# Two smaller transfers near the end, and tiles of their own for the last sums, in a decode-attention kernel

## The chip, the cores and the metric

The kernel runs on one core of a Trainium2 chip. The time is device microseconds (us) of that core; lower is better. A "run" is one timed execution. The profile is one execution with the hardware profiler on; its span is about 1.8 us shorter than the time that is reported for the same execution (1341.8 us against 1343.62 us for the kernel before).

Names: PE is TensorE, DVE is VectorE, ACT is ScalarE, SP is the engine that issues the transfers (all but one of the two of the output). Landing times come from the landing records of the trace, sixteen for a transfer; a transfer has "landed" with the last of them. L576 is line 576 of the kernel in question.

## The reference

```python
x = A_x                                          # [4, 1, 1024], bf16
g = sigmoid((x * gate_w).sum(-1, keepdims=True))
q = (x @ wq) -> [4, 32 heads, 1, 128]
p = softmax(q . k_cache * 128**-0.5)             # k_cache, v_cache: [4, 32, 8192, 128]
a = (p . v_cache) -> [4, 1, 4096] @ wo           # wo: [4096, 1024]
b = x + sigmoid(x . w_r) * (silu(x @ w_gate) * (x @ w_up)) @ w_down   # one token is chosen of one
out = g * a + (1 - g) * b
```

The two caches are 268 MB each. Everything else is small beside them.

## The kernel before

The caches are read in 32 "pairs" each, of 8 MB (four heads of one batch). A ring of five slots of 4 MB in SBUF takes them; a pair needs two slots. The order is: K pairs 0 to 31, V pair d eight places behind K pair d, and at the end the eight V pairs 24 to 31 alone, with the rows of `wo` behind them. PE multiplies each V pair in 64 matmuls into `o_ps` (four banks of PSUM). After every second V pair ACT and DVE sum the four banks into `OS`; the next pair may not overwrite `o_ps` before. `finish` then sends `OS` through eight small matmuls, and `scaled` writes the result to `OT`.

```python
    def load_pair(src, n, apart=False):
        a = slots(2)
        if a + 1 < NS and not apart:             # the two slots lie side by side: one transfer of 8 MB
            ...
            nc.sync.dma_start(out=flat[:, lo:lo + 2 * n], in_=src)
            return [...]
        for i, half in enumerate(halves):        # else two of 4 MB
            nc.sync.dma_start(out=half[:, 0:n], in_=src[:, i * n:(i + 1) * n])
...
    def v_pair(d):
        ...
        if d < ND - 1:                           # ND = 32
            vs = load_pair(vv, RING, apart=d >= ND - 3)
        else:                                    # pair 31: 2 x 2 MB and 4 x 1 MB
            vs = [ring[:, slots(1)] for _ in range(2)]
            for half, cuts in ((0, 2), (1, 4)):
                for c in range(cuts):
                    ...
        for u in range(4 * RD):                  # 16 steps of 4 matmuls
            n, z = divmod(u, 4)
            vn = vs[n // JT]
            for w in range(4):
                j0 = CJ * (n % JT) + 16 * z + 4 * w
                nc.tensor.matmul(o_ps[row:row + NM, w, :], lhsT=PB[...], rhs=vn[:, j0 * Dh:(j0 + 4) * Dh],
                                 start=(u == 0), stop=(u == 4 * RD - 1), skip_group_check=True)
            if u == 1:
                flush()                          # finish of the sums before
...
    A_ps.append(S0)      # after K pair 31: the tile of the scores, four banks, becomes
                         # output accumulators (banks 0, 1), oT (2), row sums and LT rows (3)
...
    # the end: wo blocks 2 to 7; acc(n) is bank n of A_ps[0]
    res = turned(Bn, D)
    nc.vector.tensor_copy(out=res[:, 0:NB], in_=acc(0))
    nc.sync.dma_start(out=out2[:, 0:NB], in_=res[:, 0:NB])
    nc.scalar.copy(out=res[:, NB:D], in_=acc(1))
    nc.scalar.dma_start(out=out2[:, NB:D], in_=res[:, NB:D])
```

Waits are set by the framework in which the kernel is written.

## Time and profile before

| | kernel before |
|---|---|
| median of the first 3 runs | 1345.1 us (1344.78 to 1345.45) |
| span of the profiled execution | 1341.8 us |
| HBM read, mean rate | 575.68 MB, 429 GB/s |
| PE / DVE busy | 79% / 48% |
| last landing of an input | 1337.35 us |

From the page of the kernel before, the DMA row (busy tenths in 40 slices of the span) and the total:

```profile
DMA  9999999999999999999999999999999999999997
...
HBM read 575.68 MB, written 0.01 MB: 429 GB/s over the span
```

The transfers never pause before the last slice (9 in 39 of 40), so bytes over rate set nearly the whole time. The rate by slice is 415 to 443 GB/s in those 39 and 326 GB/s in the last.

What is left to argue about is the end. The waits of PE of the kernel before, from 1235 us to the end (total us, times, longest):

```profile
PE o_ps L536 <- DMA ring<-in_A_v_cache_dram: 10.9, 4, 6.5
PE o_ps L536 <- DVE OS L556: 3.1, 1, 3.1
PE S_ps L285 <- DMA ring<-in_A_wo_dram: 1.2, 2, 0.6
PE S_ps L285 <- DVE LT L382: 0.7, 2, 0.4
PE S_ps L285 <- DVE OT L576: 0.3, 1, 0.3
```

After 1259 us PE hardly waits for data (0.9 us for pair 31 and 1.2 us for `wo`). The timeline of the kernel before over its last 15 us (start us, length, engine, line, operation; in brackets idle time before it and what ended it):

```profile
1330.34 0.24 DVE L576 SCALAR_TENSOR_TENSOR OT<-S_ps,sgb,rinv 128x8 bf16<-128x8 f32 x1 [2.93 <-PE S_ps L564]
1330.63 1.89 PE L285 MATMUL S_ps<-ring,LT 128*4 128x512 bf16 x8 [0.33 <-DVE OT L576]
1332.36 0.32 PE L380 MATMUL S_ps<-OT,identb 128*32 128x8 bf16 x16
1332.76 0.19 DVE L382 CAST LT<-S_ps 128x32 bf16<-128x32 f32 x1 [2.18 <-PE S_ps L380]
1333.00 5.34 PE L285 MATMUL S_ps<-ring,LT 128*4 128x512 bf16 x24 [0.32 <-DVE LT L382]
1338.38 0.68 DVE L622 CAST TB<-S_ps 4x512 bf16<-4x512 f32 x1 [5.43 <-PE S_ps L285]
...
1339.09 0.57 ACT L624 CAST TB<-S_ps 4x512 bf16<-4x512 f32 x1 [14.03 <-DVE TB L622]
```

PE stands 0.33 us for the scaling of `OT`; ACT copies its half of the output only after DVE.

### The profile page before, as it was taken

The page shows a single profiled execution, that of the slowest core. Times are in us where ns is not written, and L with a number is a line of the kernel's source. Part 1 is how long each engine was busy: PE and PEld are TensorE (multiplying, and loading weights), DVE is VectorE, ACT ScalarE, POOL GpSimd, SP SyncE. Part 2 cuts the span into 40 slices and gives each one's busy share as a digit, 9 for nine tenths or more (in the row PEclk, how much of TensorE's full clock was granted, in tenths as well). Part 3 has the DMA queues.
Part 4 walks back from the last instruction along what each step waited for, and adds up shares of the span by engine and source line. Part 5 has one row for each costly group of instructions (what it writes and reads, how often), then busy time and mean ns, then how long its engine had stood idle before and what let it go on. Part 6 is the DMA issues. An engine that isn't in the chain of part 4 may idle for free.

```text
span 1341.8 us, 6893 instructions
## 1 busy us (share of the span) xinstructions
PE 1055.8 (79%) x4608; PEld 138.4 (10%) x1396; DVE 639.0 (48%) x386; ACT 63.3 (5%) x94; POOL 71.4 (5%) x209
## 2 busy tenths in 40 slices
PE   2565877887788788787879778789697879887888
PEld 0000000001011010101001010101011011111111
DVE  2555988556544347455436256646145556000001
ACT  0000000200000000100000000100000000100000
POOL 2000000100000001000000000100000000100000
PEclk9777989898989899888889889889898889889999
DMA  9999999999999999999999999999999999999997
GB/s 415 438 430 435 435 438 423 443 430 424 434 436 427 443 434 422 443 428 432 438 429 434 434 432 432 436 436 424 430 433 433 436 428 442 432 421 437 426 425 326
DMA packets 14314, 576.13 MB, mean 429 GB/s; under 512 B 1598, under 2 KB 1606, under 8 KB 2252
## 3 DMA queue, kind: packets, MB, share of 16 engines
q1 hardware_dynamic: 14276, 575.69, 99.5%
q8 instruction: 23, 0.38, 0.1%
q14 instruction: 7, 0.06, 0.0%
q10 hardware_dynamic: 8, 0.00, 0.0%
HBM read 575.68 MB, written 0.01 MB: 429 GB/s over the span
## 4 chain that ended last, share of the span: by engine, by line
DMA 65%; DVE 24%; PE 11%; issue 0%; ACT 0%; SPq 0%; DVEq 0%
DMA ring<-in_A_k_cache_dram 51%; DVE TB L452 21%; PE o_ps L536 8%; DMA ring<-in_A_v_cache_dram 7%; DMA ring<-in_A_wo_dram 4%; DMA ring<-in_B_w_gate_dram 3%; DVE OS L556 2%; PE S_ps L457 1%; PE S_ps L285 1%; PE o_ps L319 0%; PE S_ps L564 0%; DVE PT L493 0%; DVE mx L479 0%; DVE OT L576 0%; ACT OS L552 0%
## 5 line engine op out<-in xcount | busy, mean ns | idle before, releaser
L452 DVE STREAM_TRANSPOSE TB<-ring 128x2048 uint32<-128x2048 uint32 x256 | 568.2, 2278 | 472.0 <-DMA ring<-in_A_k_cache_dram 453.9
L457 PE MATMUL S_ps<-TB,Z 128*128 128x512 bf16 x2048 | 531.0, 414 | 189.5 <-DVE TB L452 181.9
L536 PE MATMUL o_ps<-ring,PB 128*64 128x512 bf16 x2048 | 462.1, 388 | 52.6 <-DMA ring<-in_A_v_cache_dram 46.3
L457 PEld LDWEIGHTS <-Z 128*128 128x128 bf16 x512 | 53.0, 104 | 652.6 <-issue 652.6
L536 PEld LDWEIGHTS <-PB 128*64 128x64 bf16 x512 | 57.2, 112 | 451.7 <-issue 451.1
L556 DVE SCALAR_TENSOR_TENSOR OS<-o_ps,mE,OS 128x512 f32<-128x512 f32 x48 | 35.6, 741 | 142.1 <-ACT OS L552 141.0
L512 POOL COPY PB<-PT 32x256 bf16<-32x256 bf16 x64 | 38.9, 608 | 721.5 <-PE o_ps L536 528.5
L510 ACT COPY PB<-PT 32x256 bf16<-32x256 bf16 x64 | 39.6, 619 | 255.7 <-PE o_ps L536 249.9
L434 POOL COPY Z<-qa 32x4 bf16<-32x4 bf16 x128 | 25.6, 200 | 458.2 <-PE S_ps L457 431.0
L552 ACT ACTIVATE OS<-o_ps,mE 128x512 f32<-128x512 f32 x16 | 11.0, 687 | 584.7 <-PE o_ps L536 584.7
L488 ACT ACTIVATE TB<-S_ps,mx 128x2048 bf16<-128x2048 f32 x4 | 7.9, 1967 | 322.2 <-DVE mx L485 322.2
L285 PE MATMUL S_ps<-ring,hT 128*4 128x512 bf16 x56 | 14.6, 430 | 5.4 <-ACT TB L488 5.4
L243 PE MATMUL S_ps<-identb,x 6*128 6x6 bf16 x8 | 0.6, 195 | 22.1 <-DMA x<-in_gate_w_dram 22.1
L285 PE MATMUL S_ps<-ring,LT 128*4 128x512 bf16 x64 | 14.6, 379 | 2.3 <-DMA ring<-in_A_wo_dram 1.2
L564 PEld LDWEIGHTS o_ps<-selg,OS 128*128 128x128 f32 x88 | 11.5, 191 | 9.3 <-issue 8.8
L493 DVE STREAM_TRANSPOSE PT<-TB 128x2048 bf16<-128x2048 bf16 x4 | 9.2, 2312 | 6.4 <-ACT TB L488 6.4
L479 DVE TENSOR_REDUCE mx<-S_ps 128x1 f32<-128x2048 f32 x4 | 9.1, 2282 | 6.2 <-PE S_ps L457 6.2
L319 PE MATMUL o_ps<-ring,xw 128*4 128x512 bf16 x112 | 8.9, 442 | 3.9 <-DMA ring<-in_B_w_gate_dram 3.9
L564 PE MATMUL o_ps<-selg,OS 128*128 128x8 f32 x88 | 10.5, 245 | 0.0
L576 DVE SCALAR_TENSOR_TENSOR OT<-S_ps,sgb,rinv 128x8 bf16<-128x8 f32 x5 | 1.2, 236 | 14.6 <-PE S_ps L564 14.5
L245 DVE COPY xw<-S_ps 128x48 bf16<-128x48 bf16 x1 | 0.2, 182 | 15.6 <-PE S_ps L243 15.6
L382 DVE CAST LT<-S_ps 128x96 bf16<-128x96 f32 (+1 forms) x2 | 0.4, 224 | 14.5 <-PE S_ps L380 14.5
(68 smaller groups left out, 72.3 us busy)
## 6 DMA issues: line engine op xcount, KB each, us to landing
ring<-in_A_v_cache_dram SPq DMA_DIRECT2D x16, 4096.0 KB, 29.4
ring<-in_A_k_cache_dram SPq DMA_DIRECT2D x14, 4096.0 KB, 29.8
ring<-in_B_w_gate_dram SPq DMA_DIRECT2D x1, 7168.0 KB, 37.1
ring<-in_B_w_up_dram SPq DMA_DIRECT2D x1, 7168.0 KB, 37.1
ring<-in_B_w_down_dram SPq DMA_DIRECT2D x1, 7168.0 KB
ring<-in_A_wo_dram SPq DMA_DIRECT2D x6, 1024.0 KB, 24.7
ring<-in_A_v_cache_dram SPq DMA_DIRECT2D x2, 2048.0 KB, 32.7
ring<-in_A_v_cache_dram SPq DMA_DIRECT2D x4, 1024.0 KB, 24.6
```

What stands on the lines that cost most here:

```text
L285: nc.tensor.matmul(acc(n), lhsT=lhsT, rhs=rhs, start=start, stop=True, skip_group_check=True)
L434: nc.gpsimd.tensor_copy(out=Z[at, :, QP - 1 + QP * q], in_=qa[at, :, h0 + q, b])
L452: nc.vector.transpose(out=flat_t.bitcast(U32).rearrange("p (j i) -> p j i", j=CJ), in_=kn[:, half].bitcast(U32))
L457: nc.tensor.matmul(sps[:, z, :], lhsT=Z[:, 2 * half + e, s:s + P], rhs=T[:, 16 * z:16 * z + 16, :, e], start=(t + n + half + e == 0), stop ...
L479: nc.vector.tensor_reduce(out=mx[:, 0:1], in_=sps[:].rearrange("p z n -> p (z n)"), axis=AX.X, op=ALU.max)
L493: nc.vector.transpose(out=PT[:].rearrange("p j i -> p (j i)"), in_=PTs)
L510: nc.scalar.copy(out=Bv[at, :, :, q, :], in_=Pv[at])
L512: nc.gpsimd.tensor_copy(out=Bv[at, :, :, q, :], in_=Pv[at])
L536: nc.tensor.matmul(o_ps[row:row + NM, w, :], lhsT=PB[:, RD * (d % NW) + n, z].rearrange("p w s j -> p (w s j)"), rhs=vn[:, j0 * Dh:(j0 + 4 ...
L552: nc.scalar.activation(out=OS[:], in_=o_ps[:, 0, :], func=ACT.Copy, scale=mE[:, 0:1])
L556: nc.vector.scalar_tensor_tensor(out=OS[:], in0=o_ps[:, w, :], scalar=mE[:, w:w + 1], in1=OS[:], op0=ALU.mult, op1=ALU.add)
L564: nc.tensor.matmul(oT, lhsT=OS[:, q * Dh:(q + 1) * Dh], rhs=selg[:, q].rearrange("p t s -> p (t s)"), start=(q == 0), stop=(q == 3), skip_ ...
```

## The change

Two intents. Second halves of V pairs 29 and 30 arrive as two 2 MB transfers, so that PE may begin on them earlier. And the accumulators of the output and the small results lie in tiles of two banks each, with two result tiles, so that no instruction waits for one that uses another bank. The diff, cut:

```diff
-    scp = ctx.enter_context(tc.tile_pool(name="scp", bufs=1, space=PSUM))
+    scores = ctx.enter_context(ExitStack())
+    scp = scores.enter_context(tc.tile_pool(name="scp", bufs=1, space=PSUM))
 ...
-        lp = bank(A_ps[0], 3, [FR, n, Bn])
+        lp = bank(A_ps[1], 1, [FR, n, Bn])
 ...
-        if d < ND - 1:
-            vs = load_pair(vv, RING, apart=d >= ND - 3)
+        if d < ND - 3:
+            vs = load_pair(vv, RING)
         else:
             vs = [ring[:, slots(1)] for _ in range(2)]
-            for half, cuts in ((0, 2), (1, 4)):
+            for half, cuts in ((0, 1), (1, 2)) if d < ND - 1 else ((0, 2), (1, 4)):
 ...
-            ps = A_ps[0] if A_ps else o_ps          # in finish: oT in bank 2, tot in bank 3
+            ps = A_ps[1] if A_ps else o_ps          # oT in bank 0, tot in bank 1
 ...
-                A_ps.append(S0)
+                scores.close()
+                fin = ctx.enter_context(tc.tile_pool(name="fin", bufs=1, space=PSUM))
+                A_ps.append(fin.tile([P, NH, NB], F32, name="acc"))
+                A_ps.append(fin.tile([P, 2, NB], F32, name="led"))
 ...
-    res = turned(Bn, D)
-    nc.vector.tensor_copy(out=res[:, 0:NB], in_=acc(0))
+    res = [turned(Bn, NB) for _ in range(NH)]
+    nc.vector.tensor_copy(out=res[0], in_=acc(0))     # ACT: res[1], acc(1); each its own transfer
```

More of the change, by code (lines that the diff above doesn't have):

```diff
@@ L560, in finish @@
         def finish():
-            ps = A_ps[0] if A_ps else o_ps
-            oT = bank(ps, 2, [HV])
+            ps = A_ps[1] if A_ps else o_ps
+            oT = bank(ps, 0, [HV])
             for q in range(4):
@@ L566, in finish @@
             if t == GV - 1:
-                tot = bank(ps, 3, [GH])
+                tot = bank(ps, 1, [GH])
                 nc.tensor.matmul(tot, lhsT=rs_t[g][:, 0:1].to_broadcast([P, P]), rhs=mask, start=True, stop=True, skip_group_check=True)
@@ L620 @@
         use()
-    res = turned(Bn, D)
-    nc.vector.tensor_copy(out=res[:, 0:NB], in_=acc(0))
-    nc.sync.dma_start(out=out2[:, 0:NB], in_=res[:, 0:NB])
-    nc.scalar.copy(out=res[:, NB:D], in_=acc(1))
-    nc.scalar.dma_start(out=out2[:, NB:D], in_=res[:, NB:D])
+    res = [turned(Bn, NB) for _ in range(NH)]
+    nc.vector.tensor_copy(out=res[0], in_=acc(0))
+    nc.sync.dma_start(out=out2[:, 0:NB], in_=res[0])
+    nc.scalar.copy(out=res[1], in_=acc(1))
+    nc.scalar.dma_start(out=out2[:, NB:D], in_=res[1])
 _INS = ['A_x', 'A_k_cache', 'A_v_cache', 'A_wq', 'A_wo', 'B_x', 'B_w_r', 'B_w_gate', 'B_w_up', 'B_w_down', 'gate_w']
```

## The prediction

> **What bounds the kernel now.** Transfer. The page of the profile gives 575.7 MB read at a mean of 429 GB/s over a span of 1341.8 us, with the DMA row at 9 in every slice but the last. [...]  The landings in the trace run without a gap to the end: the second half of V pair 29 at 1278.0 us, the halves of pair 30 at 1287.7 and 1297.7, then wo and pair 31, the last piece of wo at 1337.35.
>
> **The end.** By the timeline: wo matmuls of block 3 from 1327.43; eight selector matmuls end at 1330.30; DVE scales OT until 1330.58; PE stands 0.33 us before block 4 (releaser: that DVE instruction) though block 4's data had landed at 1329.86. Then L380, the LT copy, and 24 wo matmuls 1333.00 to 1338.36 without a gap. DVE copies one half of the output 1338.38 to 1339.06, and only then ACT the other, 1339.09 to 1339.66; its transfer lands at 1340.97, the DVE's at 1340.35.
>
> **Split of pairs 29 and 30.** It lets PE begin a second half about 4.9 us earlier. PE does not wait there: pair 29's second half landed at 1278.0 and PE reaches it at about 1279.6 (64 matmuls of 0.216 us per pair, counted back from 1286.6). Pair 30 starts at 1289.74, held by the sums of pair 29 (3.13 us idle, releaser DVE OS), and arrives at its second half at about 1297.75, as it lands; the waits show no gap. PE then runs on to 1319.97, where it waits for the last pieces of pair 31 in either case. So: about 0 us gained. Cost: the two 2 MB pieces of pair 31 landed in 4.9 us each, halves of 4 MB in 9.7 us, so +0.1 us per split pair, an estimate, +0.2 in all. The extra issues make later transfers wait for the landing of earlier ones (before, two of pair 31's pieces waited so), but about 20 us of transfers are queued then; I expect no hole.
>
> **Tiles of their own.** Separate tiles for accumulators and small results take away PE's 0.33 us, if the tile is what tied them. Nearly all of it counts: with the last piece at 1337.35 to 1337.5 and two matmuls after it, PE could end no sooner than about 1338.0. Separate result tiles should let ACT copy beside DVE: that takes the ACT copy out of the chain, 0.6 to 0.7 us. [...] I give 60% that the ACT copy really moves; it may be tied through the accumulator tile, which stays one.
>
> **Sum.** -0.3 - 0.6 + 0.2 = about -0.7 us: 1344.4 us, range 1341.5 to 1346.5, mostly run and chip scatter. Faster by over 2%: 0.01; within 2%: 0.98; slower: 0.01.
>
> **What would show it.** Right: mean GB/s and the last wo landing unchanged within 1 us; no PE wait on DVE OT before block 4; the ACT copy starts within 0.1 us of the DVE copy; span after the last landing 4.45 us before, about 3.5 after. Wrong on the split: landings at the end earlier or later by more than 1 us, or new DMA gaps after 1240 us.
>
> **What would make the prediction wrong.** An earlier release of ring slots that fills holes I don't see; a wait for the old scores tile before w_down's matmuls that is longer than today's 5.4 us on ACT's exponential; the state of the chip.

The 0.216 us of a matmul are in the trace of the kernel before: the median step between the starts of the `o_ps` matmuls after 1236 us where the granted clock was 1.00. So are the two issues of pair 31 that waited for earlier landings (13.8 us in all).

## The result, and the profile after

The changed kernel took 1343.21 us in the median of 6 runs (1342.75 to 1345.62); the kernel before, in 6 runs with them, 1344.94 us (1343.53 to 1348.86). The ratio is 0.9987, 95% interval 0.9972 to 1.0003: the same within 2%, and not separable from no change.

The profiled execution of the changed kernel is, at 1345.62 us, the slowest of its six runs. That is luck for the reader, because it shows what can make a run slow. From the page after:

```profile
DMA  9999999999999999999999999999999999999997
...
HBM read 575.68 MB, written 0.01 MB: 428 GB/s over the span
```

The transfers are as they were; the last landing is at 1337.16 us (before 1337.35). The waits of PE after, over the same stretch from 1235 us to the end:

```profile
PE o_ps L537 <- DMA ring<-in_A_v_cache_dram: 7.0, 2, 3.8
PE o_ps L537 <- DVE OS L557: 3.1, 1, 3.1
PE acc L286 <- DVE LT L383: 0.4, 1, 0.4
```

The waits for `OT` and for `wo` are gone, and so are those for pair 31 (the two left are for pairs 27 and 28). The tiles explain the first. The others are gone because PE was late and found its data landed. The chain that ended last, after, in order of time:

```profile
1258.62 2.56 PE o_ps L537 x8
1261.18 1.81 PE led L565 x8
1262.98 26.52 PE o_ps L537 x120
...
1292.63 2.45 PE o_ps L537 x8
1295.08 1.81 PE led L565 x8
1296.88 14.08 PE o_ps L537 x56
...
1315.25 13.93 PE o_ps L537 x64
```

From pair 28 on no transfer is on this chain. In the kernel before the same eight matmuls took 1.89 us and the 120 took 24.82 us. The timelines show it, with the gap before each pair in brackets. The kernel before:

```profile
1258.98 1.89 PE L536 MATMUL o_ps<-ring,PB 128*64 128x512 bf16 x8 [3.44 <-DMA ring<-in_A_v_cache_dram]
...
1261.79 24.82 PE L536 MATMUL o_ps<-ring,PB 128*64 128x512 bf16 x120
1289.74 1.89 PE L536 MATMUL o_ps<-ring,PB 128*64 128x512 bf16 x8 [3.13 <-DVE OS L556]
```

and the kernel after:

```profile
1258.62 2.56 PE L537 MATMUL o_ps<-ring,PB 128*64 128x512 bf16 x8 [3.78 <-DMA ring<-in_A_v_cache_dram]
...
1292.63 2.45 PE L537 MATMUL o_ps<-ring,PB 128*64 128x512 bf16 x8 [3.14 <-DVE OS L557]
```

The windows view tells why. Columns: stretch, its length, then busy us (instructions) of PE, PEld, DVE, ACT and POOL, then the granted clock of PE, DMA share and GB/s. Two stretches of the kernel before:

```profile
1260.00:1267.00 7.00, 7.00 (x38) 1.73 (x15) 0.23 (x1) 0.00 (x0) 0.00 (x0) 1.00 1.01 435
...
1294.00:1301.00 7.00, 7.00 (x34) 0.88 (x8) 0.00 (x0) 0.00 (x0) 0.00 (x0) 1.00 0.99 415
```

and of the kernel after:

```profile
1260.00:1267.00 7.00, 7.00 (x22) 2.27 (x11) 0.23 (x1) 0.00 (x0) 0.00 (x0) 0.54 0.98 421
...
1294.00:1301.00 7.00, 7.00 (x22) 2.27 (x11) 0.23 (x1) 0.00 (x0) 0.00 (x0) 0.53 1.01 424
```

The clock records of the changed kernel show a granted clock of 0.50 in two windows of 6.8 us (from 1259.7 and 1293.8 us), "half-speed windows" in what follows; the means of 0.54 and 0.53 above include a little time at 1.00. The median step between the starts of the `o_ps` matmuls after 1236 us is 0.427 us where the records show 0.50, and 0.216 us where they show 1.00 (both traces). In its two 7 us stretches PE did 22 matmuls where it did 38 and 34 before. In both cases PE had just stood still: 3.78 us before pair 28 (waiting for its 8 MB) and 3.14 us before pair 30 (waiting for the sums of pair 29). The clock fell 1.1 and 1.2 us after PE had resumed. In these two traces the half-speed windows last 3.41, 6.83, 10.24, 13.65 or 17.07 us (but for the last of each, which the end of the trace cuts off), and the changes of the clock lie whole multiples of 3.4133 us apart, to within 1 ns from one to the next. In the 3.41 us before each of the two windows PE had been busy for 31% and 35% of the time. In the profile of the kernel before, the same gaps, 3.4 and 3.1 us, fell across two 3.41 us stretches each (counted off from a change of the clock), PE was busy for at least 48% of every one, and no window followed. That the gaps and the busy share before a window bring it about is inferred from these four cases; what sets the clock is not shown.

The end of the changed kernel, by its timeline:

```profile
1332.66 1.06 PE L565 MATMUL led<-selg,OS 128*128 128x8 f32 x8
1333.65 1.89 PE L286 MATMUL acc<-ring,LT 128*4 128x512 bf16 x8
1333.76 0.23 DVE L577 SCALAR_TENSOR_TENSOR OT<-led,sgb,rinv 128x8 bf16<-128x8 f32 x1 [1.49 <-PE led L565]
...
1340.66 0.68 DVE L626 CAST TB<-acc 4x512 bf16<-4x512 f32 x1 [4.69 <-PE acc L286]
1340.87 0.57 ACT L628 CAST TB<-acc 4x512 bf16<-4x512 f32 x1 [10.96 <-PE acc L286]
```

PE no longer stands before block 4 (1333.65), and ACT copies beside DVE, which itself starts 0.2 us before PE's last matmul ends. From PE's last matmul to the end of the span it is 2.95 us (1343.8 - 1340.85), before 3.44 us (1341.8 - 1338.36).

### The profile page after: what moved, and what is told of

Its sections match the earlier page's. It is cut to its first block, busy times and chain, and to the rows that moved or that the text cites. A ratio compares the mean times of both kernels' runs of the same rounds, so it can differ in the third digit from the quotient of the medians.

```text
span 1343.8 us, 6898 instructions
## 1 busy us (share of the span) xinstructions
PE 1063.6 (79%) x4608; PEld 139.9 (10%) x1396; DVE 638.9 (48%) x386; ACT 63.3 (5%) x94; POOL 71.6 (5%) x209
## 4 chain that ended last, share of the span: by engine, by line
DMA 59%; DVE 23%; PE 16%; another core or an unknown queue 1%; issue 0%; ACT 0%; SPq 0%; DVEq 0%
DMA ring<-in_A_k_cache_dram 51%; DVE TB L453 20%; PE o_ps L537 12%; DMA ring<-in_A_v_cache_dram 7%; DVE OS L557 2%; PE S_ps L458 2%; DMA x<-in_gate_w_dram 2%; PE acc L286 1%; PE led L565 0%; PE S_ps L320 0%; DVE PT L494 0%; DVE mx L480 0%; ACT OS L553 0%; PE o_ps L565 0%
## 5 line engine op out<-in xcount | busy, mean ns | idle before, releaser
L537 PE MATMUL o_ps<-ring,PB 128*64 128x512 bf16 x2048 | 469.7, 392 | 48.9 <-DMA ring<-in_A_v_cache_dram 39.5
L286 PE MATMUL acc<-ring,hT 128*4 128x512 bf16 x56 | 14.2, 421 | 5.4 <-ACT TB L489 5.4
L286 PE MATMUL acc<-ring,LT 128*4 128x512 bf16 x64 | 14.4, 379 | 0.4 <-DVE LT L383 0.4
```

Of the source, the lines that this page charges most:

```text
L286: nc.tensor.matmul(acc(n), lhsT=lhsT, rhs=rhs, start=start, stop=True, skip_group_check=True)
L537: nc.tensor.matmul(o_ps[row:row + NM, w, :], lhsT=PB[:, RD * (d % NW) + n, z].rearrange("p w s j -> p (w s j)"), rhs=vn[:, j0 * Dh:(j0 + 4 ...
```

## The experiments

Theory: the transfers end at about 1337.2 us whatever is done; the tiles shorten what follows; the split gives PE nothing; and PE has so little slack after pair 28 that half-speed windows show in the time. Rivals: the split brings the gain; or the transfers alone set the end, and the scatter is theirs.

### Which half of the change does what

The changed kernel again, and each half alone: `split_only` is the kernel before with only the diff of `v_pair`; `tiles_only` is the changed kernel without it.

> The changed kernel again, as the control on this chip. My theory: the transfers end at 1337.2 us in every execution, and what lies after them depends on where the half-speed windows of the TensorE clock fall after about 1258 us. Expected against the kernel before: 0.7 to 1.7 us less in the median of the fast runs (ratio 0.9987 to 0.9995). If all is scatter: ratio 0.999 to 1.001 with either sign.

> Only the two 2 MB transfers for the second halves of V pairs 29 and 30; the tiles as before. My theory: no PE instruction waits for those halves, so 0 us within 0.5 us against the kernel before (ratio 0.9996 to 1.0004), the ACT copy of the output still after the DVE copy. Rival (the split is what brings the gain, because PE resumes sooner): 1 us or more less than before, ratio 0.9993 or under.

> Only the tiles: accumulators and small results in tiles of two banks, two result tiles; the transfers of pairs 29 and 30 as before. My theory: all of the gain of the change, 0.7 to 1.0 us less than before (ratio about 0.9993 to 0.9995); in the profile no wait of PE on the scaling of OT before wo block 4, DVE and ACT copies of the output side by side. Rival (the split brings the gain): 0 us within 0.3.

| on one chip | runs | median, range (us) | ratio to before, 95% |
|---|---|---|---|
| before | 11 | 1343.51 (1343.25 to 1348.39) | |
| changed | 5 | 1343.62 (1342.55 to 1343.83) | 0.9995 (0.9983 to 1.0007) |
| split only | 6 | 1344.74 (1343.51 to 1347.56) | 1.0009 (0.9995 to 1.0023) |
| tiles only | 5 | 1342.81 (1342.50 to 1343.57) | 0.9992 (0.9980 to 1.0004) |

No interval excludes 1, and the control did not show the lower median that I expected of it (its ratio, 0.9995, is at the edge of what I wrote). For `split_only` I had expected 0 us within 0.5 us; by its ratio it was 1.2 us slower, an interval that still includes no change. The signs favour the tiles and give nothing to the split. The mechanism is clearer than the times. In `split_only` and in the profile after, the half-speed windows fell at the same times to 0.1 us, so the two can be compared directly: the spans are 1345.7 and 1343.8 us. PE began pair 28 0.32 us later in `split_only`, which no tile explains; the remaining 1.6 us are PE's two waits of 0.33 and 0.32 us, and 0.65 us in the stretch after PE's last matmul (3.60 us against 2.95 us), to within 0.3 us. In `tiles_only` the last landing is 1337.24 us and the span 1340.7 us, so 3.46 us follow it.

### Which tile

`res_only` is the kernel before with two result tiles; `banks_only` has `acc` and `led` but one result tile.

```diff
 # res_only, against the kernel before
-    res = turned(Bn, D)
+    res = [turned(Bn, NB) for _ in range(NH)]
 # banks_only, against tiles_only
-    res = [turned(Bn, NB) for _ in range(NH)]
+    res = turned(Bn, D)
```

> The kernel before with two result tiles and nothing else: read for one line of its profile. If the shared result tile made ACT wait for DVE: the ACT copy of the output starts within 0.1 us of the DVE copy. If it was the shared scores tile that both read: ACT still starts 0.7 us after DVE. In either case PE still stands 0.33 us before wo block 4 on the scaling of OT.

> The kernel before with accumulators and small results in tiles of two banks of their own, one result tile, the transfers as before. No wait of PE on the scaling of OT before wo block 4 (0.33 us before). If the shared scores tile made ACT wait for DVE: the ACT copy starts as soon as PE's last matmul ends, beside the DVE copy, and the two result tiles were not needed. If the result tile did: ACT starts 0.7 us after DVE.

The timeline of `res_only`:

```profile
1332.38 1.89 PE L285 MATMUL S_ps<-ring,LT 128*4 128x512 bf16 x8 [0.33 <-DVE OT L576]
...
1340.13 0.68 DVE L622 CAST TB<-S_ps 4x512 bf16<-4x512 f32 x1 [5.43 <-PE S_ps L285]
...
1340.84 0.57 ACT L624 CAST TB<-S_ps 4x512 bf16<-4x512 f32 x1 [12.60 <-DVE TB L622]
```

and of `banks_only`:

```profile
1330.06 1.89 PE L286 MATMUL acc<-ring,LT 128*4 128x512 bf16 x8
...
1337.67 0.68 DVE L626 CAST TB<-acc 4x512 bf16<-4x512 f32 x1 [5.29 <-PE acc L286]
1337.89 0.57 ACT L628 CAST TB<-acc 4x512 bf16<-4x512 f32 x1 [12.53 <-PE acc L286]
```

The two result tiles do nothing, and the tiles in PSUM do everything. So the layout in PSUM held ACT back. By which rule of the framework is not shown: DVE and ACT still read one tile, `acc`, after the change, so it cannot be that they shared a tile as such. What left their tile is the bank of `oT` and the bank of the row sums and `LT` rows, and the tile is a new one. `banks_only` took 1342.34 and 1342.45 us (2 runs), the lowest; `res_only` 1345.38 and 1346.05 us, with a half-speed window of 10.2 us from 1258.1 us in its profile. One profile each shows which tile it is; two runs each do not settle the time.

### Is PE short of slack?

`pe_less_28` takes 28 of the 64 matmuls of pair 28 out (wrong, though the comparison with the reference still passed it); `pe_more_28` adds 28 with zero weights, which leaves the result right. Both start from the changed kernel.

```diff
 # pe_less_28
-            for w in range(4):
+            for w in range(0 if d == ND - 4 and u % 2 == 0 and u > 0 else 4):
 # pe_more_28, after the matmuls of each step
+            for w in range(4 if d == ND - 4 and u % 2 == 0 and u > 0 else 0):
+                j0 = CJ * (n % JT) + 16 * z + 4 * w
+                nc.tensor.matmul(o_ps[row:row + NM, w, :], lhsT=none[:], rhs=vn[:, j0 * Dh:(j0 + 4) * Dh],
+                                 start=False, stop=False, skip_group_check=True)
```

> The changed kernel with 28 extra matmuls of zero weights in V pair 28, 6.05 us of PE at full clock (28 times 0.216 us), about what two half-speed windows of 6.8 us took in the profile of the changed kernel; the result stays right. My theory: PE's slack after 1258 us is about 2.5 us, so the end moves by 3 to 4 us in a run without half-speed windows there: 1346 to 1348 us; last landing unchanged. Rival (transfers alone set the end, PE has slack): within 0.5 us of the changed kernel.

> The changed kernel without 28 of the 64 matmuls of V pair 28, a wrong result on purpose: 6.05 us less for PE at full clock. My theory: this shows the floor that the transfers set: 1342.3 to 1343.0 us in every timed run, scatter under 0.7 us, whatever half-speed windows there are; PE waits for the last pieces of pair 31 and of wo. Rival (the scatter of the runs is the transfers' own): median and scatter as for the changed kernel, 1342.6 to 1345.6 us.

`pe_more_28` took 1348.80 us (1348.48 to 1349.76, 4 runs), some 5 us more than the changed kernel (4.6 us by the two ratios to the kernel before, 1.0029 and 0.9995; the changed kernel was timed on other chips), while its last landing moved only to 1338.29 us. `pe_less_28` took 1343.19 us (1342.90 to 1343.54, 4 runs), a little above the 1342.3 to 1343.0 us I expected, with the scatter as expected. Its profile had 10.2 us at half speed from 1258.1 us and 3.4 us from 1288.8 us, as much as the profile after (two times 6.8 us), and yet its span was 1341.3 us against 1343.8 us: with less work PE absorbed the windows. So PE's lateness can make a run slow, and the rival "transfers alone" falls. That it made each slow run is inferred: only one execution of a kernel has a trace, and the slowest of the kernel before (1348.86 us) has none. The added cost was above the 3 to 4 us I expected; the profile of `pe_more_28` had a window of 10.2 us at 1294.7 us, so part of it is clock. How much was not separated.

### How large may a piece be?

`whole_29_30` lets pairs 29 and 30 come as 8 MB each; `tiles_pe_more_28` puts the extra matmuls into `tiles_only` (4 MB halves), to ask whether the split helps a late PE.

```diff
 # whole_29_30, against the changed kernel
-        if d < ND - 3:
+        if d < ND - 1:
             vs = load_pair(vv, RING)
 ...
-            for half, cuts in ((0, 1), (1, 2)) if d < ND - 1 else ((0, 2), (1, 4)):
+            for half, cuts in ((0, 2), (1, 4)):
```

> The changed kernel, but V pairs 29 and 30 come as one 8 MB transfer each, coarser than before the change. My theory: halves of 4 MB were already fine enough for PE, wholes of 8 MB are not: PE starts pair 29 at 1278 instead of 1273 and pair 30 at 1297.7 instead of 1289.7, pair 31's matmuls end about 7 us later, and the end moves by about 5 us, to 1347 to 1349 us; transfers still end at 1337.2 within 1 us. Rival (the end is set by the transfers alone): 1343.2 within 0.5 us.

> The tiles alone, halves of 4 MB for pairs 29 and 30, and the 28 extra matmuls in pair 28: is the split worth something when PE is late? My theory: no, a late PE finds both halves landed: 1348.8 us within 0.8 us, as with the split. Rival (the split is insurance for a late PE): 2 us or more over that, 1351 us or more.

`whole_29_30` took 1350.87 us (1348.56 to 1351.80, 4 runs), ratio 1.0041 (1.0021 to 1.0061), a real loss. Its timeline shows PE held by the landing of both pairs:

```profile
1277.92 15.66 PE L537 MATMUL o_ps<-ring,PB 128*64 128x512 bf16 x64 [2.58 <-DMA ring<-in_A_v_cache_dram]
...
1297.38 3.59 PE L537 MATMUL o_ps<-ring,PB 128*64 128x512 bf16 x8 [3.80 <-DMA ring<-in_A_v_cache_dram]
...
1320.82 14.00 PE L537 MATMUL o_ps<-ring,PB 128*64 128x512 bf16 x64
```

So 4 MB halves bring about 6 us over 8 MB wholes: 5.5 us (0.0041 of 1344 us) against the kernel before, which has the halves but not the tiles, and 6.6 us against `tiles_only`, by two ratios taken on two chips. I expected 1347 to 1349 us; the profile also has 10.2 us at half speed from 1295.8 us, after the wait for pair 30. Halving once more brought nothing: `tiles_pe_more_28` took 1348.28 us (1346.60 to 1349.65, 4 runs), with 2 MB pieces, on another chip, it was 1348.80 us (ratios 1.0031 and 1.0029). A late PE finds both halves landed: no matmul of pairs 29 and 30 waits for them in the timeline of `tiles_pe_more_28`.

### The change carried to pairs 26 to 28

If waits for whole pairs 27 and 28 cost PE its slack, they should come in halves. `halves_from_26` cuts pairs 26 to 30 like the change does; `halves_pe_more_28` adds the 28 matmuls to it; `halves4_from_26` is `tiles_only` with 4 MB halves alone:

```diff
 # halves4_from_26, against tiles_only
-            vs = load_pair(vv, RING, apart=d >= ND - 3)
+            vs = load_pair(vv, RING, apart=d >= ND - 6)
 # halves_from_26, against the changed kernel
-        if d < ND - 3:
+        if d < ND - 6:
```

> The change carried further: V pairs 26, 27 and 28 come as 4 MB + 2 MB + 2 MB too, so that PE doesn't wait for the whole 8 MB of 27 and 28 (6.5 and 3.4 us idle before them in the profile of before). My theory: PE then runs 5 us or more ahead of where it was when pair 31's last pieces land, so a half-speed window of the clock no longer moves the end: 0.3 to 1 us less than the changed kernel in the median, and all five times within 0.8 us of each other; the last landing stays at 1337.2 within 0.5 us. Rival (the end is set by transfers alone, PE has slack already): the same median as the changed kernel within 0.2 us and the same scatter.

> The same 28 extra matmuls in the kernel in which pairs 26 to 28 come in pieces too. My theory: PE idled 3.4 us before pair 29 and 0.8 us before pair 30 there, on transfers, and takes the extra work in that idle time: 0 to 1 us over the same kernel without it, that is 1343 to 1344.3 us, 2 to 4 us under the run before this one. Rival (the pieces of 26 to 28 bring no slack): 3 to 4 us more, as in the run before.

> The tiles alone, with pairs 26 to 30 as halves of 4 MB (no 2 MB pieces there). If the start of pairs 27 and 28 on their first half is what gives PE its slack, this does as well as with 2 MB pieces: 1342.5 to 1343.3 us in the median, no run over 1344.5. If the 2 MB pieces matter once PE waits for transfers: 0.5 us or more over the kernel with them (1343.27 us), with a scatter like that of the changed kernel.

| kernel | runs | median, range (us) | last landing (us) |
|---|---|---|---|
| `halves_from_26` | 6 | 1343.27 (1342.97 to 1344.38) | 1337.66 |
| `halves_pe_more_28` | 4 | 1343.07 (1343.00 to 1344.37) | 1337.81 |
| `halves4_from_26` | 5 | 1342.68 (1342.59 to 1343.04) | 1337.22 |

Twenty-eight extra matmuls now cost nothing, where they cost some 5 us without the halves. `halves_pe_more_28` against `pe_more_28` (1343.07 and 1348.80 us, on one chip) is the cleanest pair: same extra work, only the size of earlier transfers differs. PE's timeline in `halves4_from_26`:

```profile
1250.03 2.41 PE L537 MATMUL o_ps<-ring,PB 128*64 128x512 bf16 x8 [3.13 <-DVE OS L557]
...
1278.18 8.75 PE L537 MATMUL o_ps<-ring,PB 128*64 128x512 bf16 x32 [2.65 <-DMA ring<-in_A_v_cache_dram]
...
1322.33 1.89 PE L537 MATMUL o_ps<-ring,PB 128*64 128x512 bf16 x8 [0.60 <-DMA ring<-in_A_v_cache_dram]
1324.81 1.89 PE L286 MATMUL acc<-ring,LT 128*4 128x512 bf16 x8 [0.60 <-DMA ring<-in_A_wo_dram]
```

PE starts pair 28 at 1250.03 us instead of 1258.62 us, waits for the second half of pair 29, and is again waiting for data at 1322.33 us, although this execution had windows of 6.8 us at 1251.2 us and 3.4 us at 1278.6 us. For the expectation of `halves_from_26`, the floor and the slack were as said, but the scatter was 1.4 us where I had written 0.8 us, and the median gain over the changed kernel was 0.35 us, within the scatter.

`halves4_from_26` is the version to keep: 1342.68 us against 1343.90 us (1343.33 to 1347.20, 9 runs) for the kernel before on the same chip. The ratio, 0.9990 (0.9977 to 1.0004), still includes 1, because the kernel before scatters; what looks better is that all its five runs lie within 0.45 us. No run shows it faster than `tiles_only` (1342.81 us on another chip): what its trace adds is room, since PE waits for data again near the end. 9 of 33 runs of the kernel before were over 1345 us, 1 of 11 of the changed kernel, none of the 19 runs of the four kernels that give PE slack (these three and `pe_less_28`). They ran on several chips, so this is a count and not a test. Nor does it tell slack from tiles: those four kernels have the tiles too, and the three with the tiles but without that slack (changed, `tiles_only`, `banks_only`) have 1 of 18, while `split_only` and `res_only`, without the tiles, have 5 of 8.

### What stays open

In the seven profiles with 2 MB pieces for pairs 29 and 30 the last landing was 1337.2 to 1338.4 us, mean 1337.8 us; in the six with 4 MB halves and no 2 MB pieces (the kernel before, `tiles_only`, `res_only`, `banks_only`, `tiles_pe_more_28`, `halves4_from_26`) it was 1337.1 to 1337.4 us, mean 1337.2 us. The split may thus cost some 0.5 us at the end. But `whole_29_30`, without 2 MB pieces there, had 1338.08 us too, and in that profile and in those of 1338.3 and 1338.4 us one landing record of sixteen came 1 us after the others. The cause was not settled.

## Why the prediction was right or wrong

- **Bound by transfer, last landing unchanged within 1 us:** right. 1337.35 before, 1337.16 after; 428 GB/s.
- **The split gains about 0 us:** held. The step behind it also held: no PE instruction waited for those halves, on time (`tiles_only` is not slower than the changed kernel) or late (`tiles_pe_more_28`). Its cost of +0.2 us, worked out from landing times, may be too low; 0.5 us is what the landings suggest, with the cause open.
- **The tiles save PE 0.33 us:** right, and too small by a wait. I took the 0.32 us before the last 24 matmuls for a need of data; block 5 needs nothing of that `LT` copy, and the wait went with the tile. PE's last matmul ended at 1337.89 us in `tiles_only` against 1338.34 us.
- **The ACT copy beside the DVE copy, -0.6 us, at 60%, by separate result tiles:** the effect came; the cause was wrong. `res_only` shows that the result tiles don't matter, `banks_only` that the PSUM tile does. I had feared that the accumulator tile "which stays one" might tie the two; it did not. The mark I had set, a start within 0.1 us of the DVE copy, was missed: it was 0.21 us, since DVE began before PE's last matmul had ended.
- **Sum of about -0.7 us:** in line with the data. `tiles_only` against the kernel before gives about -1.1 us by the ratio, the whole change -1.7 us by the ratio in the first rounds (0.0013 of 1344.9 us) and -0.7 us by the ratio in the second. None is separable from zero, so the size rests on the traces. My range, 1341.5 to 1346.5 us, was seven times as wide as the effect, so the measured time inside it proves little.
- **About 3.5 us after the last landing:** 3.46 us in `tiles_only` and 3.58 us in the second profile of the changed kernel (1342.0 - 1338.42), but 6.64 us in the first.
- **"PE then runs on to 1319.97, where it waits for the last pieces of pair 31 in either case":** this step failed. In the profile after, PE waited for none of them and finished 3.7 us after the last landing. In the second profile of the changed kernel it did not wait for them either, but it did wait 0.59 us for a piece of `wo`, and finished 0.65 us after the last landing. I read PE's wait of 0.36 us there as proof that PE was fast enough; it was proof that PE had 0.36 us to spare there, 2.2 us with the three waits after it (0.59, 0.60 and 0.60 us). A window of 6.8 us at a granted clock of 0.50 takes 3.4 us, an estimate from these two numbers. I wrote scatter off as "the state of the chip", when a source of it stood in the clock row. The time stayed within my range.

## What to carry to other kernels

When transfers bound a kernel, ask of the last stage how long the other engines still work after the last byte lands, and how much they may slip before that changes: a fresh PE gap of 3 us can be paid twice, once as waiting and once as half clock (here gaps of 3.78 and 3.14 us were each followed by 6.8 us at a granted clock of 0.50; in the profile before, gaps of 3.44 and 3.13 us were not). Cut transfers until the consumer waits for pieces and no longer for wholes, and begin some pairs before the end, since the slack must be earned earlier; beyond that, more cuts brought nothing here (1348.28 us with 4 MB halves, 1348.80 us with 2 MB pieces). Where two engines use different banks of one PSUM tile and wait for each other, divide the PSUM tile first: here it was the one edit of the change that showed in the trace.

## What else the traces show

- The length of a gap alone does not decide whether a half-speed window follows: a gap of 3.14 us was followed by 6.8 us at a granted clock of 0.50 (profile after, 1289.5 us) and one of 3.13 us by none (profile before, 1286.6 us). The busy share of PE differed: 31% and 35% in the 3.41 us before the two windows, at least 48% in each stretch over which the two gaps of the kernel before fell. Windows of 6.8 us come with matmuls running all through them (profile after, 1293.8 us).
- DVE and ACT copied from different banks of one PSUM tile at once (profile after: starts 0.21 us apart, 0.68 and 0.57 us long, with a right result). Where the accumulators and the small results shared one tile, PE waited 0.33 and 0.32 us for DVE though they used different banks; with two tiles neither wait is there. The wait of the ACT copy for the DVE copy, some 0.7 us, went with the same edit, by a rule that is not shown.
- The sixteen landing records of one transfer lie far apart at the end. For the last piece of `wo` in the kernel before they came from 1332.20 to 1337.35 us, seven of them over 3 us before the last, and the rate falls over the final 5 us (305 GB/s from 1332 to 1333 us, 100 GB/s from 1336 to 1337 us).
